# Moving the second layer's products two slots later, with their operands' loads and parts, in a fused attention and feed-forward kernel

## The chip, the cores and the metric

The kernel runs on one core of one Trainium2 chip. The metric is the device time of one execution in microseconds (us). Engines are called as in the profile: PE (TensorE matmuls), PEld (TensorE's weight loads), DVE (VectorE), ACT (ScalarE), POOL (GpSimd) and SP (SyncE, which issues nearly all DMAs here). `L627` is line 627 of the kernel before.

## What is computed

```python
scores = (1 / S) * z @ z.transpose(0, 2, 1)      # z: 4 x 3008 x 64
attn = np.maximum(scores, 0.0) ** 2
x = (u * (attn @ v)).reshape(12032, 256)         # u, v: 4 x 3008 x 256
gate = 1 / (1 + np.exp(-(x @ w_gate)))           # w_gate, w_val: 256 x 1536
out = (gate * (x @ w_val)) @ w_out               # w_out: 1536 x 256
```

Everything is computed to nearly full fp32 by splitting each operand into a high and a low part; a product then takes three matmuls (high by high, high by low, low by high).

## The kernel before, in words

The order of the whole program is written out by hand. There is no planner: the instructions stand on each engine in the order in which the Python code calls the helpers, and two tables put side work into that order. `before` and `after` hold side work of the attention by step number `g` (run just ahead of or behind the step's own work), and `extra` holds side work of the feed-forward part by `(J, slot)`.

**Attention, 0 to about 905 us.** 288 steps: 4 batches, 6 chunks of queries (512, the last 448), 12 pairs of key blocks; `per` = 72 steps are one batch. A step takes scores on PE (L343, L344), squares them on ACT, makes a high part `ah` (ACT, L367) and a low part `al` (DVE, L372) and multiplies with v (`pe_pv`, L487 to L494). As scores are symmetric, some steps don't compute them but load those of an earlier step, which were transposed on DVE and stored to DRAM (`store_turned`, L398, L403; `load_back`, L461, issued five steps ahead). All of these DMAs go through SP's one queue, in program order. Beside the steps run: the next batch's z (`load_z`, `turn_z` on DVE two steps later, `z_high` on ACT at L262 and `z_low` on DVE at L266 one step after that); 18 `Narrow` jobs that prepare the weights and store them to DRAM (L227); the stores of attention's result, `keep` (copy L512, DMA L510). In the last batch (g from 216 on) the feed-forward part's first operands are fetched too: `load_w` (L604, 896 KB each), `load_sums` (L545), `load_u` (L556, eight DMAs each), `turn_u` and `make_x` (DVE).

**Feed-forward, from about 891 us.** 12 groups `G` of 1024 tokens (the last of 768), `NF` = 6 pairs of blocks of the hidden width; `J` = 6 G + F numbers the 72 blocks. A block has a gate half and a value half. Each half is seven products of Strassen's scheme (`pe_product`, L627 to L629, three matmuls each, in the order P1, P6, P2, P7, P5, P4, P3), which go round the PSUM banks 0 to 3. A block has eight slots, 0 to 7, after P6, P7, P5 and P3 of the gate half and then of the value half. In each slot `beside(J, slot)` puts one product of the second layer (`pe_out`, L685 to L687, three matmuls) of the block before, in the order of the quarters 11, 22, 21, 12, twice each, and then what `extra` holds for the slot. So a block is 42 + 24 = 66 matmuls.

The other engines serve a block in this order. ACT: `copy_s1` (L646) out of PSUM, sigmoids (`gate`, L656), the high parts of the hidden values (`h_high`, L664). DVE: `join` (L652), which adds PSUM banks up and frees them. POOL: `gated` (gate times value, L660) and the low parts of the hidden values (`h_low`, L669). The quarters 22, 21 and 12 of a block are finished early in the next block: `h_low(J-1, 22)` is called before that block's P6 (its operand shows as `al` or `al_69`).

Each group prepares the next one's operand beside its blocks: `load_sums`, `load_u` (L556), `turn_u` (DVE L565), `make_x` (DVE L573), four differences `sum_x` (DVE L583), four high parts `x_high` (ACT L587) and four low parts `x_low` (DVE L592), the last of them in the slots 0 to 3 of the group's sixth block. `finish` (DVE L693, DMA L696) writes a group's output. The second layer's weights come by `load_o` (L611, 512 KB), the value halves' weights by `load_w(J + 2, 1)` ahead of each block.

Of the kernel before, what the change touches and what calls it, by code (L numbers as in the profile page):

```python
# [26 lines left out]
def kernel(  # L27
# [20 lines left out]
    NF = DFF // (2 * P)  # L48
# [652 lines left out]
    with tc.manual_schedule():  # L701
# [13 lines left out]
        for b in range(1, B):  # L715
            g0 = (b - 1) * per
            for p in range(NCH):
# [5 lines left out]
                at(before, g + 3, z_high, b, p)  # L723
                at(before, g + 3, z_low, b, p)
# [12 lines left out]
        starts = [24, 31, *range(84, 127, 7), *range(156, 199, 7), 221, 228]  # L737
# [9 lines left out]
        at(after, g + 2, load_w, 0, 1)  # L747
        at(after, g + 6, load_w, 1, 1)
        for t in range(2):
            at(after, g + 10 + t, load_sums, 0, t)  # L750
        for t in range(2):
            at(after, g + 14 + 10 * t, load_u, 0, t)
            at(before, g + 20 + 10 * t, turn_u, 0, t)
            at(before, g + 21 + 10 * t, make_x, 0, t)
        for J in range(3):
            at(after, g + 28 + 5 * J, load_w, J, 0)
# [108 lines left out]
        for G in range(1, len(groups) + 1):  # L865
            J = (G - 1) * NF
            if G < len(groups):
                for t in range(2):
                    at(extra, (J, 0), load_sums, G, t)
                line = (  # L870
                    (1, 3, load_u, 0), (1, 7, turn_u, 0), (1, 7, load_u, 1), (2, 3, make_x, 0), (2, 7, turn_u, 1),
                    (3, 3, make_x, 1), (3, 4, x_high, B1), (3, 7, x_low, B1),
                    (4, 0, sum_x, T1), (4, 1, sum_x, T3), (4, 3, sum_x, T2), (4, 4, sum_x, T4),
                    (4, 5, x_high, T12), (4, 7, x_low, T12), (5, 0, x_high, T34), (5, 1, x_low, T34),
                    (5, 2, x_high, B2), (5, 3, x_low, B2),
# [3 lines left out]
                for x, (t, h) in enumerate(((0, 0), (0, 1), (1, 0), (1, 1))):  # L879
                    at(extra, (J + NF + (x == 3), (5, 6, 7, 0)[x]), finish, G - 1, t, h)  # L880
        at(extra, (0, -1), load_o, 0)
        at(extra, (0, 1), load_w, 2, 1)
        for J in (3, 4, 5):
            at(extra, (0, 7), load_w, J, 0)
        at(extra, (0, 7), keep, *steps[-1][:2], False)
        at(extra, (0, 7), keep, *steps[-1][:2], True)
        for F in range(1, NF):
            at(extra, (0, 7), load_o, F)
# [8 lines left out]
        def attention():  # L897
            for s in steps[-2:]:
                yield from pe_pv(s)

        other = attention()
# [5 lines left out]
        for J in range(last + 1):  # L907
            run(extra, (J, -1))
            for value in range(2):
# [20 lines left out]
                if J and not value:  # L930
                    h_high(J - 1, 12)
                    h_low(J - 1, 12)
# [4 lines left out]
                beside(J, k + 1)  # L937
                pe_product(J, value, "P5", S1, T12, 0)
# [18 lines left out]
            other = outs(J)  # L957
        gated(last, 12)
        for c in (22, 21, 12):
# [37 lines left out]
```

## Time and profile before

| | us |
|---|---|
| median of 3 runs | 1933.91 (1931.49 to 1935.72) |
| the profiled execution's own time | 1938.98 |
| its span | 1937.2 |

| engine | busy us | share of the span |
|---|---|---|
| PE | 1895.7 | 98% |
| PEld | 1659.7 | 86% |
| DVE | 1514.5 | 78% |
| ACT | 1151.5 | 59% |
| POOL | 765.4 | 40% |

PE is busy nearly always; the mean granted clock of the span is 0.997. A busy share says little here about where the rest is: the waits of PE stand in few places, and the rows further down show them one by one. In a row of the timeline the first number is the start in us from the span's start, the second the duration of one instruction, `x2` the number of instructions drawn together, and the square bracket the idle time just before with what ended it.

### The profile page before, as it was taken

The page shows a single profiled execution, that of the slowest core. Times are in us where ns is not written, and L with a number is a line of the kernel's source. Part 1 is how long each engine was busy: PE and PEld are TensorE (multiplying, and loading weights), DVE is VectorE, ACT ScalarE, POOL GpSimd, SP SyncE. Part 2 cuts the span into 40 slices and gives each one's busy share as a digit, 9 for nine tenths or more (in the row PEclk, how much of TensorE's full clock was granted, in tenths as well). Part 3 has the DMA queues.
Part 4 walks back from the last instruction along what each step waited for, and adds up shares of the span by engine and source line. Part 5 has one row for each costly group of instructions (what it writes and reads, how often), then busy time and mean ns, then how long its engine had stood idle before and what let it go on. Part 6 is the DMA issues. An engine that isn't in the chain of part 4 may idle for free.

```text
span 1937.2 us, 26164 instructions
## 1 busy us (share of the span) xinstructions
PE 1895.7 (98%) x8870; PEld 1659.7 (86%) x8870; DVE 1514.5 (78%) x1946; ACT 1151.5 (59%) x1504; POOL 765.4 (40%) x609
## 2 busy tenths in 40 slices
PE   9999999999999999999899999999999999999998
PEld 7888988888887988889788888888888888888898
DVE  7687688887888797657678787888878787888876
ACT  8886788767886787764344444444444444444443
POOL 3000000000000000002577677777777677777675
PEclk9999999999999999999999999999999999999999
DMA  6679589997899889966342515243442415242331
GB/s 141 144 204 245 161 191 238 253 266 197 203 245 272 250 211 219 271 192 241 98 112 87 122 59 142 80 104 92 104 111 89 115 65 142 79 105 86 99 98 36
DMA packets 596726, 298.77 MB, mean 154 GB/s; under 512 B 529904, under 2 KB 547056, under 8 KB 596592
## 3 DMA queue, kind: packets, MB, share of 16 engines
q1 hardware_dynamic: 591312, 294.48, 57.4%
q0 software_dynamic: 1024, 2.10, 0.5%
q8 instruction: 69, 1.13, 0.2%
q10 hardware_dynamic: 4256, 0.52, 0.2%
q14 instruction: 65, 0.53, 0.1%
HBM read 189.92 MB, written 101.06 MB: 150 GB/s over the span
## 4 chain that ended last, share of the span: by engine, by line
PE 77%; POOL 5%; DVE 4%; issue 4%; DMA 3%; ACT 3%; SPq 3%; DVEq 0%; ACTq 0%; POOLq 0%
PE banks L494 10%; PE banks L487 9%; PE banks L627 9%; PE banks L489 9%; PE banks L629 9%; PE banks L628 9%; PE banks L686 5%; PE banks L687 5%; PE banks L685 5%; POOL keep L660 3%; PE banks L344 3%; PE banks L343 3%; DMA r<-shared 2%; DVE al L372 1%; ACT ah L367 1%
## 5 line engine op out<-in xcount | busy, mean ns | idle before, releaser
L660 POOL TENSOR_TENSOR keep<-keep,spare 128x512 f32<-128x512 f32 (+1 forms) x284 | 377.1, 1339 | 1069.2 <-DVE keep L652 1069.2
L372 DVE TENSOR_TENSOR al<-r,ah 128x1024 fp32r<-128x1024 f32 (+1 forms) x287 | 341.2, 1191 | 181.0 <-ACT ah L367 175.3
L487 PE MATMUL banks<-ah,v 128*128 128x512 f32 (+1 forms) x1152 | 429.5, 376 | 9.6 <-ACT ah L367 9.3
L489 PE MATMUL banks<-ah,v 128*128 128x512 f32 (+1 forms) x1104 | 414.0, 375 | 0.0
L494 PE MATMUL banks<-al,v 128*128 128x512 f32 (+1 forms) x1152 | 341.2, 378 | 5.8 <-DVE al L372 4.0
L367 ACT ACTIVATE ah<-r 128x1024 fp32r<-128x1024 f32 (+1 forms) x251 | 255.9, 1034 | 69.7 <-DMA r<-shared 36.6
L487 PEld LDWEIGHTS banks<-ah,v 128*128 128x128 f32 x1152 | 218.0, 189 | 39.0 <-ACT ah L367 13.1
L494 PEld LDWEIGHTS banks<-al,v 128*128 128x128 f32 x1152 | 215.7, 189 | 40.9 <-DVE al L372 15.9
L652 DVE TENSOR_TENSOR zt<-banks,zt 128x512 f32<-128x512 f32 (+1 forms) x288 | 193.4, 672 | 71.7 <-ACT zt L646 66.8
L664 ACT ACTIVATE h<-keep 128x512 fp32r<-128x512 f32 (+1 forms) x144 | 89.7, 623 | 256.2 <-POOL keep L660 252.8
L656 ACT ACTIVATE spare<-spare 128x512 f32<-128x512 f32 (+1 forms) x288 | 176.0, 619 | 99.0 <-DVE spare L652 94.7
L489 PEld LDWEIGHTS banks<-ah,v 128*128 128x128 f32 x1104 | 209.0, 189 | 24.3
L669 POOL TENSOR_TENSOR h<-keep,h 128x512 fp32r<-128x512 f32 (+1 forms) x144 | 196.9, 1368 | 56.8 <-ACT h L664 56.8
L351 ACT ACTIVATE r<-banks 128x1024 f32<-128x1024 f32 (+2 forms) x173 | 167.1, 966 | 86.0 <-PE banks L344 84.5
L652 DVE TENSOR_TENSOR spare<-banks,zt 128x512 f32<-128x512 f32 (+1 forms) x288 | 188.1, 673 | 19.4 <-PE banks L629 18.4
L352 ACT ACTIVATE r<-r 128x1024 f32<-128x1024 f32 (+2 forms) x173 | 174.4, 1008 | 5.5
L646 ACT ACTIVATE zt<-banks 128x512 f32<-128x512 f32 (+1 forms) x144 | 84.1, 584 | 144.2 <-PE banks L629 138.8
L627 PE MATMUL banks<-z,v 128*128 128x512 f32 x378 | 144.1, 381 | 1.1 <-DVE zt L652 1.1
L629 PE MATMUL banks<-z,v 128*128 128x512 f32 x378 | 143.5, 380 | 0.0
L664 ACT ACTIVATE v<-keep 128x512 fp32r<-128x512 f32 (+1 forms) x144 | 89.1, 619 | 71.6 <-POOL keep L660 69.5
L343 PE MATMUL banks<-zq,z 128*128 128x512 f32 (+2 forms) x348 | 126.9, 367 | 1.4 <-DVE zq L787 1.4
L344 PE MATMUL banks<-zq,z 128*128 128x512 f32 (+2 forms) x348 | 126.8, 367 | 0.0
(156 smaller groups left out, 3785.8 us busy)
## 6 DMA issues: line engine op xcount, KB each, us to landing
v<-w_gv SPq DMA_DIRECT2D x75, 896.0 KB, 4.7
r<-shared SPq DMA_DIRECT2D x72, 512.0 KB, 5.1
shared<-turned SPq DMA_DIRECT2D x236, 128.0 KB, 2.9
r<-shared SPq DMA_DIRECT2D x38, 448.0 KB, 5.2
shared<-spare SPq DMA_DIRECT2D x128, 128.0 KB, 3.4
out_dram<-turned SPq DMA_DIRECT2D x176, 64.0 KB, 1.9
w_gv<-w SPq DMA_DIRECT2D x24, 448.0 KB, 4.1
sums<-keep SPq DMA_DIRECT2D x20, 512.0 KB, 4.4
```

The lines of the kernel that those rows point to most:

```text
L343: nc.tensor.matmul(sc[:, j, 0 : n - q0], h, q, start=True, stop=False)
L344: nc.tensor.matmul(sc[:, j, 0 : n - q0], l, q, start=False, stop=True)
L367: nc.scalar.activation(ah[:, :, 0:n], r[:, :, 0:n], AF.Copy)
L372: nc.vector.tensor_tensor(al[:, :, 0:n], r[:, :, 0:n], f32(ah[:, :, 0:n]), op=ALU.subtract)
L487: nc.tensor.matmul(o, vh[:, j, ds], moving(ah[:, j, 0:n]), start=(k == 0 and j == 0), stop=False)
L489: nc.tensor.matmul(o, vl[:, j, ds], moving(ah[:, j, 0:n]), start=False, stop=False)
L494: nc.tensor.matmul(acc[:, d, 0:n], vh[:, j, ds], moving(al[:, j, 0:n]), start=False, stop=stop)
L627: nc.tensor.matmul(o, wt[:, 0, w], xh, start=True, stop=False)
L629: nc.tensor.matmul(o, wt[:, 1, w], xh, start=False, stop=True)
L652: nc.vector.tensor_tensor(to[:, 0:m], bank(J, value, name), s_t[other][:, 0:m], op=ALU.add)
L660: (nc.vector if J == last else nc.gpsimd).tensor_tensor(y, y, g, op=ALU.mult)
L669: nc.gpsimd.tensor_tensor(lo[:, 0:m], y_t[c][:, 0:m], f32(hi[:, 0:m]), op=ALU.subtract)
```

## The change

All edits move calls; no instruction of the computation is added or removed. They are:

1. The products of the second layer of block J stand in the slots from (J+1, 2) to (J+2, 1), before in (J+1, 0) to (J+1, 7). Ten of them are left behind the last block, before eight; two of these go ahead of the last block's high and low parts. `h_high` and `h_low` of quarter 12 move behind slot 1, and `finish` moves by two slots.
2. In the group before, `load_u`, `turn_u`, `make_x` and the high and low parts of x are spread differently: a high part now stands two slots ahead of its low part or more, and `load_u`'s second half stands four slots later.
3. `load_o(F)` stands in (F-1, 7), and `load_w(F, 0)` of F = 3, 4, 5 in (0, 7), (1, 7), (2, 7); before, all eight stood in (0, 7).
4. In the last batch the two last `Narrow` jobs start at steps 246 and 261 (before 221, 228), `load_u` at 243 and 252 (before 230, 240), and the loads of weights and sums later too.
5. `z_high` and `z_low` of the next batch's z stand one step later.

```diff
@@ -720,8 +720,8 @@
                     g = 5 * NPAIR + 3
                 at(after, g, load_z, b, p)
                 at(before, g + 2, turn_z, b, p)
-                at(before, g + 3, z_high, b, p)
-                at(before, g + 3, z_low, b, p)
+                at(before, g + 4, z_high, b, p)
+                at(before, g + 4, z_low, b, p)
             line = [number[b - 1, NCH - 1, i] for i in range(NPAIR)]
             for i in range(1, NPAIR):
                 line[i] = max(line[i], line[i - 1] + 1)
@@ -734,7 +734,7 @@
             for p in range(NCH):
                 if (b, p) != (0, 0):
                     at(after, b * per + NPAIR * p - 10, z_both, b, p)
-        starts = [24, 31, *range(84, 127, 7), *range(156, 199, 7), 221, 228]
+        starts = [24, 31, *range(84, 127, 7), *range(156, 199, 7), 246, 261]
         for n, g in enumerate(starts):
             job = Narrow(n)
             at(after, g - 3, job.load)
@@ -744,16 +744,16 @@
 
 
         g = 3 * per
-        at(after, g + 2, load_w, 0, 1)
-        at(after, g + 6, load_w, 1, 1)
+        at(after, g + 3, load_w, 0, 1)
+        at(after, g + 9, load_w, 1, 1)
         for t in range(2):
-            at(after, g + 10 + t, load_sums, 0, t)
+            at(after, g + 22 + t, load_sums, 0, t)
         for t in range(2):
-            at(after, g + 14 + 10 * t, load_u, 0, t)
-            at(before, g + 20 + 10 * t, turn_u, 0, t)
-            at(before, g + 21 + 10 * t, make_x, 0, t)
+            at(after, g + 27 + 9 * t, load_u, 0, t)
+            at(before, g + 33 + 9 * t, turn_u, 0, t)
+            at(before, g + 34 + 9 * t, make_x, 0, t)
         for J in range(3):
-            at(after, g + 28 + 5 * J, load_w, J, 0)
+            at(after, g + 55 + 3 * J, load_w, J, 0)
         g = len(steps) - NPAIR
         for i in (T1, T3):
             at(before, g + 2, sum_x, 0, i)
@@ -868,24 +868,23 @@
                 for t in range(2):
                     at(extra, (J, 0), load_sums, G, t)
                 line = (
-                    (1, 3, load_u, 0), (1, 7, turn_u, 0), (1, 7, load_u, 1), (2, 3, make_x, 0), (2, 7, turn_u, 1),
-                    (3, 3, make_x, 1), (3, 4, x_high, B1), (3, 7, x_low, B1),
-                    (4, 0, sum_x, T1), (4, 1, sum_x, T3), (4, 3, sum_x, T2), (4, 4, sum_x, T4),
-                    (4, 5, x_high, T12), (4, 7, x_low, T12), (5, 0, x_high, T34), (5, 1, x_low, T34),
-                    (5, 2, x_high, B2), (5, 3, x_low, B2),
+                    (1, 4, load_u, 0), (2, 3, turn_u, 0), (2, 3, load_u, 1), (2, 7, make_x, 0), (3, 3, turn_u, 1),
+                    (3, 7, make_x, 1), (4, 0, sum_x, T1), (4, 1, x_high, B1), (4, 1, sum_x, T3), (4, 3, x_low, B1),
+                    (4, 4, sum_x, T2), (4, 5, x_high, T12), (4, 5, sum_x, T4), (4, 7, x_low, T12),
+                    (5, 0, x_high, T34), (5, 1, x_high, B2), (5, 3, x_low, T34), (5, 5, x_low, B2),
                 )
                 for dj, slot, f, x in line:
                     at(extra, (J + dj, slot), f, G, x)
                 for x, (t, h) in enumerate(((0, 0), (0, 1), (1, 0), (1, 1))):
-                    at(extra, (J + NF + (x == 3), (5, 6, 7, 0)[x]), finish, G - 1, t, h)
+                    at(extra, (J + NF + (x > 0), (7, 1, 2, 3)[x]), finish, G - 1, t, h)
         at(extra, (0, -1), load_o, 0)
         at(extra, (0, 1), load_w, 2, 1)
-        for J in (3, 4, 5):
-            at(extra, (0, 7), load_w, J, 0)
         at(extra, (0, 7), keep, *steps[-1][:2], False)
         at(extra, (0, 7), keep, *steps[-1][:2], True)
         for F in range(1, NF):
-            at(extra, (0, 7), load_o, F)
+            at(extra, (F - 1, 7), load_o, F)
+        for x, F in enumerate((3, 4, 5)):
+            at(extra, (x, 7), load_w, F, 0)
 
         def outs(J):
 
...
-        def attention():
+        def others():
+
             for s in steps[-2:]:
                 yield from pe_pv(s)
-
-        other = attention()
+            yield
+            yield
+            for J in range(last + 1):
+                yield from outs(J)
+
+        other = others()
...
-                if J and not value:
-                    h_high(J - 1, 12)
-                    h_low(J - 1, 12)
                 pe_product(J, value, "P7", S3, T34, 0)
                 join(J, value, "P7", "u3", "u2")
                 if value:
                     h_low(J, 11)
                 beside(J, k + 1)
+                if J and not value:
+                    h_high(J - 1, 12)
+                    h_low(J - 1, 12)
...
-            other = outs(J)
         gated(last, 12)
+        for _ in range(2):
+            next(other)
```

**SP's queue at the start of the feed-forward part**, before. `w_gv` and `w_o` are the prepared weights in DRAM, `sums` attention's result, `in_u_dram` the input u:

```order
L611 DMA x<-w_o 128x1024
L545 DMA turned<-sums 128x2x512 x2
L604 DMA v<-w_gv 128x1792 x4
L510 DMA sums<-turned 256x1x448
L611 DMA ah<-w_o 128x1024 x3
L611 DMA al<-w_o 128x1024 x2
L604 DMA v<-w_gv 128x1792
L556 DMA turned<-in_u_dram 32x16x32 x16
```

And now:

```order
L611 DMA x<-w_o 128x1024
L545 DMA turned<-sums 128x2x512 x2
L604 DMA v<-w_gv 128x1792
L510 DMA sums<-turned 256x1x448
L611 DMA ah<-w_o 128x1024
L604 DMA v<-w_gv 128x1792 x2
L556 DMA turned<-in_u_dram 32x16x32 x8
L611 DMA ah<-w_o 128x1024
L604 DMA v<-w_gv 128x1792 x2
L556 DMA turned<-in_u_dram 32x16x32 x8
L611 DMA ah<-w_o 128x1024
```

Counted from the first L604, the first eight loads of u stood behind eleven transfers of 448 to 896 KB (five L604, the store L510, five L611); now they stand behind five (three L604, the store, one L611).

**SP's queue in the last batch, second chunk of queries**, before. `shared` and `half` are transposed scores in DRAM, stored by L398 and loaded back by L461 and L454:

```order
L270 DMA zq<-z 64x512
L271 DMA zq<-z 64x512
L556 DMA zt<-in_u_dram 32x16x32 x8
L398 DMA shared_1_3_5660<-turned 32x16x64 x8
L461 DMA r<-shared_0_1_5272 128x1024
L454 DMA r<-half_1_5568 128x2x256
```

And now:

```order
L270 DMA zq<-z 64x512
L271 DMA zq<-z 64x512
L398 DMA shared_1_3_5630<-turned 32x16x64 x8
L461 DMA r<-shared_0_1_5272 128x1024
L454 DMA r<-half_1_5553 128x2x256
```

The eight loads of u that stood ahead of a load of transposed scores are gone from here; the first of them now stand in the third chunk.

**PE in a group's sixth block (J = 5)**, before, from slot 1 to slot 2. `z`, `zq` are the parts of x, `v` the first layer's weights; L685 to L687 are one product of the second layer, whose operands are a quarter of h (`h`, or `v` with `al_69`) and the weights `al`:

```order
L685 MATMUL banks<-h,al 128x512
L686 MATMUL banks<-h,al 128x512
L687 MATMUL banks<-h,al 128x512
L627 MATMUL banks<-z,v 128x512
L628 MATMUL banks<-z,v 128x512
L629 MATMUL banks<-z,v 128x512
L685 MATMUL banks<-v,al 128x512
L686 MATMUL banks<-al_69,al 128x512
L687 MATMUL banks<-v,al 128x512
```

And now, from slot 3 to slot 4:

```order
L685 MATMUL banks<-h,al 128x512
L686 MATMUL banks<-h,al 128x512
L687 MATMUL banks<-h,al 128x512
L627 MATMUL banks<-z,v 128x512
L628 MATMUL banks<-z,v 128x512
L629 MATMUL banks<-z,v 128x512
L627 MATMUL banks<-z,v 128x512
L628 MATMUL banks<-z,v 128x512
L629 MATMUL banks<-z,v 128x512
L685 MATMUL banks<-v,al 128x512
L686 MATMUL banks<-al_69,al 128x512
L687 MATMUL banks<-v,al 128x512
```

The product that reads `al_69`, quarter 22's low part, stood behind P5 of the gate half; it now stands behind P6 of the value half, 18 matmuls later.

## Rows read from the trace of the kernel before

**Rows 1.** Waits view, PE, whole span: line, releaser; us in total, times, longest.

```profile
PE banks L487 <- ACT ah L367: 9.3, 8, 2.7
PE banks L686 <- POOL al L669: 8.0, 11, 0.8
PE banks L627 <- DVE zt L652: 7.9, 11, 5.7
```

**Rows 2.** Timeline, PE, a value half without waits: its first matmul and the next block's.

```profile
1008.69 0.38 PE L627 MATMUL banks<-v 128*128 128x512 f32 x1
...
1015.81 0.38 PE L627 MATMUL banks<-v,wgv 128*128 128x512 f32 x1
```

**Rows 3.** Timeline, start of the feed-forward part: SP's issues, DVE, PE.

```profile
908.69 2.54 SPq L611 DMA_DIRECT2D ah<-w_o  x3
...
916.06 18.31 SPq L556 DMA_DIRECT2D turned<-in_u_dram  x16
...
929.07 1.25 DVE L565 STREAM_TRANSPOSE turned<-turned 128x1024 f32<-128x1024 f32 x1 [8.83 <-DMA turned<-in_u_dram]
...
930.94 0.79 PE L627 MATMUL banks<-z,wgv 128*128 128x512 f32 x1 [5.66 <-DVE zt L652]
```

**Rows 4.** Windows: PE, PEld, DVE, ACT, POOL busy (count), PE clock, DMA share, GB/s.

```profile
750.00:760.00 10.00, 7.12 (x24) 5.36 (x23) 5.54 (x5) 6.65 (x8) 0.00 (x0) 0.83 1.03 255
910.00:920.00 10.00, 10.00 (x48) 8.75 (x47) 7.02 (x11) 3.69 (x6) 5.87 (x6) 1.00 1.00 380
920.00:930.00 10.00, 5.28 (x25) 4.29 (x23) 1.17 (x2) 1.75 (x3) 5.85 (x5) 0.97 0.64 153
930.00:940.00 10.00, 9.06 (x30) 7.48 (x31) 7.73 (x12) 3.60 (x6) 2.14 (x2) 0.69 0.60 144
```

**Rows 5.** Timeline, PE around a group end, J = 5, and the same place a group later.

```profile
971.49 0.38 PE L627 MATMUL banks<-z,v 128*128 128x512 f32 x1
...
977.22 0.48 PE L686 MATMUL banks<-al,al 128*128 128x512 f32 x1 [0.81 <-POOL al L669]
...
980.74 0.48 PE L627 MATMUL banks<-z,v 128*128 128x512 f32 x1 [0.23 <-DVE zt L652]
...
1068.09 0.48 PE L627 MATMUL banks<-x,v 128*128 128x512 f32 x1 [0.22 <-DVE zt L652]
```

**Rows 6.** Timeline, POOL, ACT and DVE in the same block J = 5.

```profile
972.43 3.50 POOL L660 TENSOR_TENSOR keep<-keep,spare 128x512 f32<-128x512 f32 x2
975.89 1.28 POOL L669 TENSOR_TENSOR al<-keep,v 128x512 fp32r<-128x512 f32 x1
...
976.50 1.04 ACT L587 ACTIVATE x<-turned 128x1024 fp32r<-128x1024 f32 x1
...
977.58 1.91 DVE L592 TENSOR_TENSOR x<-turned,x 128x1024 fp32r<-128x1024 f32 x1 [1.93 <-ACT x L587]
```

**Rows 7.** Timeline, POOL and ACT in a block in the middle of a group, J = 8.

```profile
1015.51 2.51 POOL L660 TENSOR_TENSOR keep<-keep,spare 128x512 f32<-128x512 f32 x2
1017.98 1.28 POOL L669 TENSOR_TENSOR al<-keep,v 128x512 fp32r<-128x512 f32 x1
...
1020.53 0.63 ACT L664 ACTIVATE v<-keep 128x512 fp32r<-128x512 f32 x1 [0.50 <-POOL keep L660]
```

**Rows 8.** Timeline, last batch, second chunk: SP's issues and PE.

```profile
737.16 5.75 SPq L556 DMA_DIRECT2D zt<-in_u_dram  x8
...
747.63 0.57 SPq L461 DMA_DIRECT2D r<-shared  x1
...
753.77 0.48 PE L487 MATMUL banks<-ah,v 128*128 128x512 f32 x1 [2.75 <-ACT ah L367]
```

**Rows 9.** Timeline, PE's waits behind the last block.

```profile
1926.52 0.43 PE L686 MATMUL banks<-al,al 128*128 128x384 f32 x1 [0.43 <-POOL al L669]
...
1928.84 0.43 PE L686 MATMUL banks<-h,al 128*128 128x384 f32 x1 [0.84 <-POOL h L669]
```

**Rows 10.** Timeline, ACT, one of the 18 high parts of z.

```profile
170.85 0.61 ACT L262 ACTIVATE z<-zt 128x512 fp32r<-128x512 f32 x1
```

## Prediction

> **What bounds the kernel now.** PE: the table gives it 98% of the span, so only two things can shorten the run, idle time of PE and matmuls that run at less than the full clock. I read the waits view of PE first [rows 1]: three kinds of wait make 25.2 us, and two of the three have a longest one that is far above their mean, so they are single places and not something in every block. Then the spacing of matmuls without waits: a value half is 33 matmuls and takes 1015.81 - 1008.69 = 7.12 us, 0.2158 us each [rows 2]. With this spacing each place can be priced by its loss of matmuls, refill and clock included, not by the wait alone.
>
> *The start of the feed-forward part.* PE stands 5.66 us at 930.94 for a join of DVE. That join stands behind DVE's transpose of u (L565 at 929.07), which was idle 8.83 us for the DMA of u [rows 3]. The u was late because its 16 transfers were issued from 916.06 on, behind the weights that SP had begun to issue by 908.69. Behind the wait PE's granted clock is 0.69 in the mean of 930 to 940, so part of that stretch ran at 1.2 GHz instead of 2.4. By count: 25 + 30 matmuls in 920 to 940 where the full stretch before has 48 in 10 us [rows 4], so 96 - 55 = 41 are missing, 41 x 0.2158 = **8.8 us**.
>
> *The ends of groups.* The same matmul stands at 980.74 and, one group later, at 1068.09 [rows 5]: 87.35 us for 6 x 66 = 396 matmuls, which without waits would take 396 x 0.2158 = 85.45. So 1.90 us are lost in each group. The rows in the group's sixth block show where: L686 waits 0.81 for POOL's low part of quarter 22, and P6 of the value half waits 0.23 for DVE [rows 5]; the other 0.86 I take for the refill behind these waits, since a block without them loses nothing [rows 2]. Of the 8.0 us for which L686 waits on POOL [rows 1] 0.43 stands behind the last block [rows 9]; 7.6 / 0.81 = 9.4 full waits, 9.4 x 1.90 = **17.8 us** in all.
>
> *The last batch.* PE stands 2.75 us at 753.77 for ACT, which had waited for transposed scores; SP issued their load only at 747.63, behind eight loads of u that took it 5.75 us from 737.16 on [rows 8]. 750 to 760 holds 24 matmuls at a mean clock of 0.83 [rows 4] instead of 10 / 0.2158 = 46.3: 22 x 0.2158 = **4.8 us**.
>
> **The change part by part.**
>
> *Weights and u at the start.* The order of SP shows the first eight loads of u behind five transfers, before behind eleven; the six that went are two of 896 KB and four of 512 KB, 3.8 MB. At 380 GB/s, the rate of 910 to 920 [rows 4], that is 10 us. DVE got its data at 929.07, so they can now be there at about 919 to 922. The transposition moves too, from slot 7 of the group's second block to slot 3 of its third, that is four slots or 7.1 us later, so the data have 7 us and more before anyone waits. With DVE's idle time of 8.83 us gone, its join at 930.94 is on time. The loss goes whole: **-8.8**. Nothing takes its place in this stretch that the rows show; what moved behind u are weights that are needed one to four blocks (14.2 us each) later. Bounds: -8.8 and, if u came 4 us late once more, about -4.
>
> *The second layer's products two slots later.* In the sixth block POOL finishes the low part of quarter 22 at 975.89 + 1.28 = 977.17, 5.68 us after the block's start at 971.49 [rows 5, 6]. Its first reader stands behind 21 matmuls: due at 22 x 0.2158 = 4.75, hence the wait. In the new order that reader stands behind the value half's P6: 39 matmuls, due at 40 x 0.2158 = 8.63. The cover is 8.63 - 5.68 = 2.95 us. In the middle of a group the same part is done 1017.98 + 1.28 - 1015.81 = 3.45 us after the start [rows 7], where it had 1.30 us of cover and gets 5.2. So the wait on POOL goes.
>
> *High parts of x two slots ahead.* The wait of 0.23 on DVE stands behind a low part (L592, 1.91 us at 977.58) that had itself waited 1.93 us for ACT's high part (L587, 1.04 us at 976.50) [rows 6]. Now the high part is called two slots or four ahead, a slot being some 1.8 us, so the 1.93 us go and DVE is that much earlier than the 0.23 it lacked. The cost is ACT's: two high parts of 1.04 us stand in slots 0 and 1 of the sixth block instead of 0 and 2, ahead of the copy of P1 that DVE needs for its join. What is late next there is that copy. I can't read its lateness from the rows of before; bounds are 0 and the old small wait with its refill, 0.6 per end. I take 0.35, the nearer to the rows with such a wait: 10 x 0.35 = 3.5. Together with the products: **-17.8 + 3.5 = -14.3**.
>
> POOL was slow in this block: its two products took 3.50 us, in the middle of a group 2.51 [rows 6, 7]. These 0.99 us stay, since a low part of x still runs beside them; they are inside the 5.68. The Trainium skill, "SBUF — State Buffer", section "Who interferes with whom", has a rule that speaks against the change here: a DVE instruction with two SBUF inputs and a GpSimd instruction that reads SBUF exclude each other for the whole instruction, and the one that issued first wins. By that rule each of the low parts and differences may hold POOL once; the trace agrees in kind (3.50 against 2.51). As one more such instruction now stands in the fifth block, the sum by the rule would be worse only if its holds add up beyond the cover; that is the first rival.
>
> *The last batch.* The eight loads of u are gone from ahead of the late load [rows 8], and nothing stands in their place in SP's queue in that chunk. So the load that was issued at 747.63 comes up to 5.75 us earlier, against a wait of 2.75: **-4.8**. The same eight DMAs and the sums now stand in the third and fourth chunk. There I bound them from below by 0 and from above by one more stall like the one that goes, 4.8. I take +1.2, a quarter, for these and for the moved weights and `Narrow` jobs, nearer to 0 because one wait of 2.75 is by far the longest of its eight [rows 1], so other chunks with as many DMAs don't stall.
>
> *z a step later.* 18 high parts of 0.61 us on ACT [rows 10] and as many low parts on DVE move by one step; nothing needs them soon, so the moves themselves cost nothing. Where the new step already has ACT late, 0.61 is added to PE's wait for `ah`. Bounds: 0 and 18 x 0.61 = 11. PE waits for ACT's `ah` in eight places only [rows 1]; I take one of them in each of three batches, once whole and twice by half: **+1.1**.
>
> *Behind the last block.* Two more products, 6 matmuls of 384 columns, are put ahead of the waits of 0.43 and 0.84 [rows 9]. They fill most of the 1.27 us: **-1.0**; the chain on POOL ends it, so no more than 1.27.
>
> Sum: -8.8 - 14.3 - 4.8 + 1.2 + 1.1 - 1.0 = -26.6. The profiled execution took 1938.98, so it would take 1912.4. That execution lay 5.1 above the median of 1933.91; taken off the median, the sum gives 1907.3. **Forecast: 1907 us.**
>
> **The rivals.**
>
> *1. POOL stays the bound at group ends.* The order of the fifth and sixth block still puts six or seven two-input DVE instructions beside POOL's work. If three more of them than now hold POOL for about 0.99 us each, the low part comes 2.97 us later and the cover of 2.95 is used up; from there on each hold shows in PE. Half of the 17.8 would stay: 1907 + 5.4 (8.9 instead of 3.5) = 1912, all of it 1921. Against it: in the rows one hold of 0.99 is all that the block has. This is the page's rule worked out as a mechanism of this kernel.
>
> *2. The u loads stall another chunk.* In the third or fourth chunk of the last batch the eight DMAs (5.75 us of SP) push a load of scores as they did at 737. Each such stall costs 4.8: one gives 1911, two 1915. For it: the queue is the same. Against it: fewer stores stand there.
>
> *3. Slower: ACT waits for PE in every block.* `h_high` of quarter 12 overwrites an operand that PE now reads in slots 0 and 1 of the same block, for the block before. These products end behind 18 matmuls, 3.9 us after the block's start; the high part starts 1020.53 - 1015.81 = 4.72 after it [rows 7], so 0.8 us of margin. If ACT came to be held there by more than the later work of ACT can absorb, three sigmoids and the copy of P1 would be late and PE would wait in each of about 70 blocks. To eat up the gains it must cost 30 / 70 = 0.43 us per block; at 0.7 per block the time is 1907 + 49 = 1956. Against it: the margin is positive, and ACT is busy 59%.
>
> *4. The change doesn't do what it says.* If the join at 930.94 and the group ends were held by something beside POOL and u, both would stay: about 1931. The order shows the products and the loads moved as described, and the rows name POOL and the DMA with no other engine late, so this is small.
>
> **How the numbers follow.** Chances: forecast 0.76, first rival 0.10, second 0.06, third 0.04, fourth 0.04. The range should leave out at most 2 in 10. Its upper end takes in the second rival twice and most of the first: 1919. Its lower end: all 17.8 gone without the 3.5, nothing lost in z and the moved loads (2.3), gives 1907.3 - 5.8 = 1901.5, and with 3 us for the spread of the three runs 1898. A change of about 0.2%, 4 us, is what a measurement of this kernel can tell from none. Faster by more: forecast and rivals one and two, 0.92; within: 0.04; slower: 0.04.
>
> **What would show it.** In the waits of PE: no wait of 5 us near 930 and a clock of 1.00 in 920 to 940; L686 no longer waiting on POOL at the ends of groups, a period of 85.5 to 85.9 us between like matmuls of two groups; P6's wait on DVE below 0.3. In the last batch: no wait of 2 us or more for `ah` near 753 and none new in the two chunks after it. Wrong would be the forecast if the period stayed above 86.5, if L487 waited for ACT by more than 8 us in all, or if a wait of a few tenths stood in every block.

## The result

The changed kernel takes 1912.55 us (median of 4 runs, 1910.79 to 1913.78) where the kernel before takes 1934.82 (4 runs, 1931.49 to 1938.16): a ratio of 0.9884, with an interval of 0.9865 to 0.9904, so 22.3 us less. The forecast was 1907, the range 1898 to 1919. The profiled execution took 1912.1, its span is 1910.3, 26.9 less than the span of before.

PE's waits of the changed kernel (line, releaser; us in total, times, longest), which answer to [rows 1]:

```profile
PE banks L487 <- ACT ah L367: 6.0, 5, 2.1
...
PE banks L686 <- POOL h L669: 0.8, 1, 0.8
```

L627 on DVE (7.9 us before) and L686 on POOL in the groups (7.6 us before) are gone; what is left on POOL is the one wait behind the last block. The windows that answer to [rows 4]:

```profile
750.00:760.00 10.00, 10.00 (x48) 8.81 (x48) 4.58 (x5) 8.90 (x10) 0.00 (x0) 1.00 0.93 234
...
920.00:930.00 10.00, 10.00 (x48) 8.78 (x47) 8.65 (x13) 3.27 (x7) 5.75 (x6) 1.00 0.62 159
930.00:940.00 10.00, 10.00 (x49) 8.75 (x48) 8.48 (x12) 5.07 (x9) 7.49 (x6) 1.00 0.65 263
```

Both bad stretches are full: 48 or 49 matmuls at a granted clock of 1.00 where 24, 25 and 30 stood. The timeline shows why at the start of the feed-forward part [rows 3]; u's first half is issued 9.83 us earlier (5.9 us earlier counted from the first matmul of the feed-forward part, which stands at 888.19 here and at 892.09 before), and its transposition has no idle time ahead:

```profile
904.42 0.96 SPq L604 DMA_DIRECT2D v<-w_gv  x2
906.23 8.06 SPq L556 DMA_DIRECT2D turned<-in_u_dram  x8
...
922.08 1.23 DVE L565 STREAM_TRANSPOSE turned<-turned 128x1024 f32<-128x1024 f32 x1
```

At a group's end, J = 11, with the fifth block, J = 10, ahead of it, PE and POOL [rows 5, 6]:

```profile
1036.87 0.38 PE L629 MATMUL banks<-v 128*128 128x512 f32 x1
1037.24 0.48 PE L627 MATMUL banks<-x,v 128*128 128x512 f32 x1
...
1044.26 0.38 PE L629 MATMUL banks<-v 128*128 128x512 f32 x1
1044.61 0.48 PE L627 MATMUL banks<-x,v 128*128 128x512 f32 x1
...
1052.70 0.38 PE L686 MATMUL banks<-al,al 128*128 128x512 f32 x1
...
1123.32 0.48 PE L627 MATMUL banks<-z,v 128*128 128x512 f32 x1
```

```profile
1044.80 3.51 POOL L660 TENSOR_TENSOR keep<-keep,spare 128x512 f32<-128x512 f32 x2
1048.27 1.28 POOL L669 TENSOR_TENSOR al<-keep,v 128x512 fp32r<-128x512 f32 x1
```

POOL is as slow as before (3.51 against 3.50), its low part is ready at 1049.55, and PE reads it only at 1052.70: 3.15 us of cover, 2.95 by the prediction. Like matmuls of two groups are 1123.32 - 1037.24 = 86.08 us apart, before 87.35, and 85.45 would be without any loss. The period that the prediction gave was 85.5 to 85.9. The remaining 0.6 stand mostly in two places of like size: P6 of the fifth block's value half follows the matmul ahead of it after 0.37 us instead of 0.22 (1036.87 to 1037.24) and P6 of the sixth block's gate half after 0.35 (1044.26 to 1044.61); the matmul behind each comes 0.32 later, so each place loses some 0.25.

### The profile page after: what moved, and what is told of

The parts are those of the page before. It is cut to its first block, busy times and chain, and to the rows that moved or that the text cites. A ratio compares the mean times of both kernels' runs of the same rounds, so it can differ in the third digit from the quotient of the medians.

```text
span 1910.3 us, 26147 instructions
## 1 busy us (share of the span) xinstructions
PE 1889.4 (99%) x8870; PEld 1662.3 (87%) x8870; DVE 1531.9 (80%) x1946; ACT 1145.5 (60%) x1504; POOL 778.6 (41%) x609
## 4 chain that ended last, share of the span: by engine, by line
PE 90%; ACT 2%; SPq 2%; DVE 2%; DMA 2%; issue 1%; DVEq 0%; POOL 0%; ACTq 0%
PE banks L627 11%; PE banks L628 11%; PE banks L629 11%; PE banks L494 11%; PE banks L487 10%; PE banks L489 10%; PE banks L686 6%; PE banks L687 6%; PE banks L685 6%; PE banks L344 3%; PE banks L343 3%; DMA r<-shared 1%; SPq L252 1%; ACT ah L367 1%; DVE al L372 1%
## 5 line engine op out<-in xcount | busy, mean ns | idle before, releaser
L660 POOL TENSOR_TENSOR keep<-keep,spare 128x512 f32<-128x512 f32 (+1 forms) x284 | 387.3, 1374 | 1036.1 <-DVE keep L652 1032.0
L669 POOL TENSOR_TENSOR h<-keep,h 128x512 fp32r<-128x512 f32 (+1 forms) x144 | 188.1, 1307 | 56.8 <-ACT h L664 56.8
L652 DVE TENSOR_TENSOR spare<-banks,zt 128x512 f32<-128x512 f32 (+1 forms) x288 | 188.2, 674 | 22.5 <-PE banks L629 21.4
L627 PE MATMUL banks<-z,v 128*128 128x512 f32 x378 | 144.4, 382 | 0.0
```

The lines of the kernel that those rows point to most:

```text
L627: nc.tensor.matmul(o, wt[:, 0, w], xh, start=True, stop=False)
L652: nc.vector.tensor_tensor(to[:, 0:m], bank(J, value, name), s_t[other][:, 0:m], op=ALU.add)
L660: (nc.vector if J == last else nc.gpsimd).tensor_tensor(y, y, g, op=ALU.mult)
L669: nc.gpsimd.tensor_tensor(lo[:, 0:m], y_t[c][:, 0:m], f32(hi[:, 0:m]), op=ALU.subtract)
```

## Experiments

The kernels were compared with the kernel before on the same chip; its medians there were 1934.6 to 1935.6. Experiments one to four each do one part of the change alone.

**The products two slots later, alone.** The edit is the generator `others` with its two empty slots, the parts of quarter 12 behind slot 1, and:

```diff
-at(extra, (J + NF + (x == 3), (5, 6, 7, 0)[x]), finish, G - 1, t, h)
+at(extra, (J + NF + (x > 0), (7, 1, 2, 3)[x]), finish, G - 1, t, h)
```

> The kernel before with the second layer's products two slots later (and the finish and quarter 12's parts that go with them), nothing else of the change. Theory: POOL's late low part is the cause of the loss at group ends, so the waits of L686 on POOL (10 of 0.8 us) go and of the 1.90 us per group only P6's wait on DVE with its refill stays, about 0.5; with the tail 14 us less than before, about 1921. Rival: DVE is as late as POOL there, so PE only reaches P6 earlier and the wait of L627 on DVE grows from 0.23 to about 1.3 per group; then no more than 5 us are won, 1930 or more. The wait of 5.7 us at 931 stays in both.

Measured: 1953.3, ratio 1.0100 (1.0072 to 1.0129). It is 18.7 us slower. PE's waits, the same place at two group ends, and the third block:

```profile
PE banks L627 <- DVE zt L652: 29.6, 21, 5.2
```

```profile
978.25 0.48 PE L627 MATMUL banks<-z,v 128*128 128x512 f32 x1 [1.37 <-DVE zt L652]
...
1019.53 0.48 PE L627 MATMUL banks<-x,wgv 128*128 128x512 f32 x1 [0.87 <-DVE zt L652]
...
1066.79 0.48 PE L627 MATMUL banks<-x,v 128*128 128x512 f32 x1 [1.38 <-DVE zt L652]
```

The wait of L686 on POOL in the groups is gone, as the first theory said, but at the group's end nothing is won: P6 now waits 1.37 us for DVE instead of 0.23, as the rival said. Neither had foreseen the third block, where a new wait stands. DVE there, in this run and then in the kernel before, and SP in this run:

```profile
1017.66 1.25 DVE L565 STREAM_TRANSPOSE turned<-turned 128x1024 f32<-128x1024 f32 x1 [4.03 <-DMA turned<-in_u_dram]
```

```profile
1016.90 1.25 DVE L565 STREAM_TRANSPOSE turned<-turned 128x1024 f32<-128x1024 f32 x1 [0.79 <-DMA turned<-in_u_dram]
```

```profile
1003.88 7.59 SPq L696 DMA_DIRECT2D out_dram<-turned  x12
1011.52 11.44 SPq L556 DMA_DIRECT2D turned<-in_u_dram  x16
```

The later products make `finish` later (its first quarter by two slots, the other three by three), and the twelve stores of these three stand right ahead of u's loads in SP's queue. Counted from the group's first matmul, the loads are issued at 26.7 us (1011.52 - 984.83), before at 21.4 (1008.75 - 987.32). So u comes late, and DVE idles 4.03 us instead of 0.79. With both waits the group takes 1066.79 - 978.25 = 88.54 us.

**The operands of x, alone.** The edit is the table of `load_u` to `x_low`.

> The kernel before with u's loads, its transposition, the differences and the high and low parts of x at their new slots, nothing else. Theory: at group ends P6's wait on DVE goes (0.5 us with its refill, 10 times) and L686's wait on POOL stays at 0.8, so 5 us less there. At the start of the feed-forward part u lands no earlier than before (929), but its transposition is due four slots or 7.1 us later, at about the time at which the data are there, so the wait of 5.7 us falls under 1.5 and the clock stays up: 7 to 8.5 us less. In all about 1921. Rival: the weights ahead in SP's queue are what counts, and u stays late: a wait of 4 us or more on DVE's transposition near 930 stays, and the time is about 1929.

Measured: 1926.0, ratio 0.9958 (0.9945 to 0.9970), 8.6 us less; the profiled execution took 1928.5. PE and DVE:

```profile
971.14 0.48 PE L686 MATMUL banks<-al,al 128*128 128x512 f32 x1 [0.62 <-POOL al L669]
...
1057.99 0.48 PE L686 MATMUL banks<-al,al 128*128 128x512 f32 x1 [0.61 <-POOL al L669]
```

```profile
929.99 1.25 DVE L565 STREAM_TRANSPOSE turned<-turned 128x1024 f32<-128x1024 f32 x1 [0.19 <-DMA turned<-in_u_dram]
```

P6's wait is gone and POOL's stays; the group takes 86.85 us, 0.5 less than before, as expected. The wait at 931 is gone too, although u comes hardly earlier (transposed at 929.99, 35.5 us behind the first matmul of the feed-forward part, before at 929.07, 37.0 behind it): with its use four slots later DVE is idle for 0.19 us instead of 8.83. At the prices read from the profiled execution of before these two would be 13 us, and 1921 was expected; the median shows 8.6. The next experiment prices the second of them lower, which is most of the rest.

**The weights spread, alone.** The edit:

```diff
-for J in (3, 4, 5):
-    at(extra, (0, 7), load_w, J, 0)
...
-    at(extra, (0, 7), load_o, F)
+    at(extra, (F - 1, 7), load_o, F)
+for x, F in enumerate((3, 4, 5)):
+    at(extra, (x, 7), load_w, F, 0)
```

> The kernel before with the second layer's weights and three of the first layer's spread over the blocks, nothing else. Theory: u's loads stand behind five transfers instead of eleven and land about 10 us earlier (919 to 922), DVE's idle time of 8.8 us goes, the wait of 5.7 us goes with its half clock: 8.5 us less, about 1926. Rival: the weights share the DMA engines with u either way, u comes less than 4 us earlier, and 3 us or more of the wait stay. The group ends keep their 1.9 us each in both.

Measured: 1929.6, ratio 0.9970 (0.9958 to 0.9982), 5.1 us less. DVE's transposition:

```profile
923.31 1.25 DVE L565 STREAM_TRANSPOSE turned<-turned 128x1024 f32<-128x1024 f32 x1 [0.95 <-DMA turned<-in_u_dram]
```

u is transposed 5.8 us earlier than before (929.07), or 7.9 us earlier counted from the first matmul of the feed-forward part (894.21 here, 892.09 before), and that suffices: no wait of PE is left there. The gain is smaller than the forecast, though: 8.5 us less were expected, and 5.1 came, with 3.5 to 8.1 in the interval. So either the spread of the weights or the later use of u cures the start of the feed-forward part by itself, the changed kernel has both, and the whole wait is worth less in the medians than the 8.8 us read from one trace.

**The last batch, alone.** The edit is the new steps of `load_w`, `load_sums`, `load_u`, `turn_u`, `make_x` and of the two last `Narrow` jobs.

> The kernel before with the last batch's loads and the two last Narrow jobs at their new steps, nothing else. Theory: the wait of 2.75 us at 754 and its half clock go (4.8 us), so do the 0.44 at 809 and its refill (1.1), and one new wait of 0.9 us near 850 comes: 5 us less, about 1929. Rival: u's loads stall one of the two later chunks: a new wait of 2 us or more for ah between 780 and 880, and no gain.

Measured: 1931.8, ratio 0.9979 (0.9968 to 0.9991), 2.9 us less. The window that was bad, and the start of the feed-forward part:

```profile
750.00:760.00 10.00, 10.00 (x48) 8.83 (x47) 5.90 (x6) 8.29 (x9) 0.00 (x0) 1.00 0.89 232
```

```profile
921.86 0.79 PE L627 MATMUL banks<-z,wgv 128*128 128x512 f32 x1 [3.68 <-DVE zt L652]
```

The stall near 754 is gone, and neither of the two later chunks has one of 2 us; the rival falls. The new wait of 0.9 us near 850 did not come. At the start of the feed-forward part, where SP's queue has the same order as before, PE waits 3.68 us, before 5.66. The stall near 754 was not the same in each execution: in the three runs above, which keep the old last batch, PE's wait there was 2.97, 3.71 and 3.46 us, and in two below 1.30 and 2.56. The 2.75 us of the prediction's trace lie in the middle of these, so the term was right in place, and its size varies with the execution.

**Products and u.** The products later, and u's loads, transposition and product at their new slots, but the parts of x at their old ones:

```diff
-(1, 3, load_u, 0), (1, 7, turn_u, 0), (1, 7, load_u, 1), (2, 3, make_x, 0), (2, 7, turn_u, 1),
-(3, 3, make_x, 1), (3, 4, x_high, B1), (3, 7, x_low, B1),
+(1, 4, load_u, 0), (2, 3, turn_u, 0), (2, 3, load_u, 1), (2, 7, make_x, 0), (3, 3, turn_u, 1),
+(3, 7, make_x, 1), (3, 4, x_high, B1), (3, 7, x_low, B1),
```

> The kernel before with the products two slots later and u's loads, transposition and product four slots later, but the differences and the high and low parts of x at their old slots. In the run with the products alone two waits of L627 on DVE stood in each group: 1.4 us at the group's end, and 0.4 to 2.4 in its third block, where DVE was idle 4.0 us for u. Theory: they are two things. The third block's goes, since u gets four slots more; the group's end keeps its 1.4 us, which hang on the high part that ACT makes only one slot ahead of the low part; with the start of the feed-forward part cured too (8.5) the time is about 1925, and like matmuls of two groups lie 87.2 us or more apart. Rival: both come from the late u, the group's end gets within 0.6 of 85.45, and the time is about 1913.

Measured: 1953.4, ratio 1.0090 (1.0069 to 1.0111). One group of PE's timeline:

```profile
953.07 0.48 PE L627 MATMUL banks<-z,v 128*128 128x512 f32 x1 [0.63 <-DVE spare L652]
956.60 0.48 PE L627 MATMUL banks<-z,v 128*128 128x512 f32 x1 [1.31 <-DVE zt L652]
972.47 0.48 PE L627 MATMUL banks<-z,v 128*128 128x512 f32 x1 [1.36 <-DVE zt L652]
```

DVE ahead of the same waits a group later (PE's stand there at 1042.63 and 1046.15):

```profile
1036.24 1.83 DVE L573 TENSOR_TENSOR turned<-turned 128x1024 f32<-128x1024 f32 x1
1038.00 2.29 DVE L592 TENSOR_TENSOR z<-turned,z 128x1024 fp32r<-128x1024 f32 x1
```

The third block's wait is gone and the group's end keeps its 1.36, so these are two things, as the theory said. The time of 1925 was wrong all the same, for a reason that this edit itself made: the product by u and B1's low part now stand in the same slot, right ahead of two differences; DVE has no idle time there, and PE waits for it twice in the fifth block (953.07 and 956.60).

**Products and all operands.** The two parts together; weights, last batch and z as before.

> The kernel before with the products later and all of u's and x's operands at their new slots; second layer's weights, last batch and z as before. Theory: these two parts make the whole gain of the feed-forward part, which each of them alone does not: group period 86.1 as in the changed kernel, no wait at its start; only the last batch's stall of some 5 us is left, so 1916 to 1918. Rival: the weights' spread is needed too, and a wait of 2 us or more is left between 915 and 935: 1920 or more.

Measured: 1914.8, ratio 0.9893 (0.9870 to 0.9916). PE's waits on DVE:

```profile
PE banks L627 <- DVE zt L652: 1.3, 2, 1.0
```

Both stand in the first group: 1.00 us at 929.53 and 0.33 in the sixth block (961.50). From the second group on no wait on POOL or DVE is left, but for the one on POOL behind the last block. The theory is borne out (1916 to 1918 expected, the time 1 us lower): two parts that are worth +18.7 and -8.6 alone are worth -20.8 together.

**The parts of x one slot apart again.** The changed kernel with:

```diff
-(5, 0, x_high, T34), (5, 1, x_high, B2), (5, 3, x_low, T34), (5, 5, x_low, B2),
+(5, 0, x_high, T34), (5, 1, x_low, T34), (5, 2, x_high, B2), (5, 3, x_low, B2),
```

> The changed kernel with one thing put back: in a group's sixth block each low part of x stands one slot behind its high part again (T34 in slots 0 and 1, B2 in slots 2 and 3). Theory: the other half of the loss at group ends is DVE, which stands idle for ACT's high part while PE waits for DVE; so P6's wait of 1.4 us with its refill is back at each end, a period of 87.3, 12 us more than the changed kernel, 1924. Rival: what made the difference was the less dense order of the differences in the fifth block; then the wait stays away and the time is 1912 to 1914.

Measured: 1926.0, ratio 0.9946 (0.9926 to 0.9967), 13.4 us above the changed kernel's 1912.55 (12.0 by the two ratios). PE, then DVE and ACT:

```profile
967.84 0.48 PE L627 MATMUL banks<-z,v 128*128 128x512 f32 x1 [1.12 <-DVE zt L652]
...
1055.22 0.48 PE L627 MATMUL banks<-x,v 128*128 128x512 f32 x1 [1.13 <-DVE zt L652]
```

```profile
964.67 1.92 DVE L592 TENSOR_TENSOR x<-turned,x 128x1024 fp32r<-128x1024 f32 x1 [0.99 <-ACT x L587]
966.51 0.68 DVE L652 TENSOR_TENSOR spare<-banks,spare 128x512 f32<-128x512 f32 x1
967.11 0.68 DVE L652 TENSOR_TENSOR zt<-banks,zt 128x512 f32<-128x512 f32 x1
```

```profile
963.60 1.04 ACT L587 ACTIVATE x<-turned 128x1024 fp32r<-128x1024 f32 x1
```

The wait is back and the group takes 87.38 us. The chain can be read off: ACT's high part ends at 964.64, DVE's low part waits for it and takes 1.92, two joins follow, and PE's P6 waits for the bank that the second frees.

**The products one slot later instead of two.** The changed kernel with one empty slot in `others`:

```diff
 yield from pe_pv(s)
-yield
 yield
 for J in range(last + 1):
```

> The changed kernel with the second layer's products one slot later than before instead of two. By the prediction's sum quarter 22's low part is ready 5.68 us after the block's start and is now due behind 30 matmuls, at 31 x 0.2158 = 6.69: a cover of 1.0 us, so no wait of L686 on POOL and the same time as the changed kernel, 1912. Rival: POOL is held by more in the denser order of DVE (more two-input instructions beside it), the low part comes later than 6.7, and waits on POOL are back at group ends: 0.5 us or more each with refill, 1918 or more.

Measured: 1918.9, ratio 0.9914 (0.9891 to 0.9938); the profiled execution took 1915.9. POOL and PE in the sixth block:

```profile
961.58 1.28 POOL L669 TENSOR_TENSOR al<-keep,v 128x512 fp32r<-128x512 f32 x1
```

```profile
964.34 0.38 PE L686 MATMUL banks<-al,al 128*128 128x512 f32 x1
```

Ready at 962.86, read at 964.34: 1.48 us of cover where 1.0 was expected, and no wait on POOL. So one slot is enough against POOL. The time is not that of the changed kernel, though: PE stands idle for 0.13 us ahead of L685 at 990.97, until DVE's `finish` has ended (0.71 us from 990.21), as `finish` kept its place while its reader came a slot earlier, and like matmuls of two groups, 990.97 and 1077.53, are 86.56 us apart. Ten groups, from the first matmul of block 6 to that of block 66, take 863.0 us in this profiled execution and 859.7 in that of the changed kernel. These 3.3 us are about half of the difference of the medians; where the rest stands is not settled.

**z at its old step.** The changed kernel with `g + 3` for `z_high` and `z_low`.

> The changed kernel with z's parts back at their old step. Theory of the prediction: the later z costs 1.1 us, so 1.1 less than the changed kernel, 1911.4. First rival: it costs more, since in the changed kernel a wait of 0.9 us is new at 380 and those at 401 and 622 are 0.2 longer: 2 to 3 us less, about 1910. Second rival: it gains, since waits of 1.2 us at 446 and of 0.5 at 404 and 626 are gone there: 2 to 3 us more, about 1915.

Measured: 1912.6, ratio 0.9878 (0.9859 to 0.9896).

> The changed kernel once more, beside the others of this call: 1912.5 within 1.5.

Measured, beside it: 1911.2, ratio 0.9872 (0.9850 to 0.9894). So the step of z makes no difference that these runs can tell; the two rivals of 2 to 3 us either way aren't borne out.

**DVE's side work spread further.** The changed kernel with z at its old step and `make_x` of the first half in slot 6 instead of 7, and this table behind it:

```diff
+(2, 7, x_high, B1), (3, 1, x_low, B1), (3, 3, turn_u, 1), (3, 5, make_x, 1), (3, 6, x_high, B2), (4, 0, x_low, B2),
+(4, 2, sum_x, T1), (4, 4, sum_x, T3), (4, 6, sum_x, T2), (4, 7, x_high, T12), (5, 0, sum_x, T4),
+(5, 1, x_low, T12), (5, 2, x_high, T34), (5, 4, x_low, T34),
```

> The changed kernel with z's parts at their old step and DVE's side work for the next operand spread further: B2's parts in the fourth and at the start of the fifth block, T1, T3 and T2 two slots apart, T4 in the sixth. Theory: what the changed kernel still loses per group (86.08 against 85.45 us) are joins of DVE in the fifth block that come late behind a product and two differences in four slots; one such piece in every two slots leaves DVE time for its joins, the 0.6 us go in each of 11 groups, 6 us less than the changed kernel, 1906. Rival: the pieces meet POOL's work at their new places, DVE is late there, and the time is 1912 or more.

Measured: 1922.0, ratio 0.9928 (0.9910 to 0.9946), 9.4 us above the changed kernel with z at its old step (1912.6): the rival's time. PE waits for DVE again in the sixth block:

```profile
PE banks L627 <- DVE keep L652: 2.5, 10, 0.2
```

This wait stands in the value half, behind T34's low part, which now has the slot ahead of that join:

```profile
1143.10 1.22 DVE L592 TENSOR_TENSOR x<-turned,x 128x1024 fp32r<-128x1024 f32 x1
1144.23 0.69 DVE L652 TENSOR_TENSOR keep<-banks,zt 128x512 f32<-128x512 f32 x1
```

```profile
1144.97 0.48 PE L627 MATMUL banks<-z,v 128*128 128x512 f32 x1 [0.25 <-DVE keep L652]
```

The value half's P6 waits too in some groups, up to 0.64 us (at 965.33), for joins that stand behind T12's low part (2.34 us at 961.74, with POOL at work).

**The product by u earlier.** The changed kernel with two calls moved:

```diff
-(3, 7, make_x, 1), (4, 0, sum_x, T1),
+(3, 5, make_x, 1), (3, 7, sum_x, T1),
```

> The changed kernel with x's second product by u two slots earlier (from slot 7 to slot 5 of the fourth block) and the first difference T1 one slot earlier (slot 7 of the fourth block). Theory: the 0.6 us that the changed kernel still loses per group stand in the fifth block, where DVE works off that product, which met POOL there (1.84 us), and three differences without idle time; between them and slot 5 DVE has idle time and POOL none to give, so DVE's backlog is some 1.8 us less, the group period falls from 86.1 to about 85.6, and the time by 4 to 5 us, 1907 to 1908. Rival: DVE's backlog in the fifth block is made by the differences and the joins alone; the period stays at 86, the time at 1912.

Measured: 1908.0 (1906.2 to 1909.3), ratio 0.9854 (0.9837 to 0.9871). Like matmuls two groups apart:

```profile
1062.69 0.38 PE L628 MATMUL banks<-zq,wgv 128*128 128x512 f32 x1
...
1233.63 0.38 PE L628 MATMUL banks<-zq,wgv 128*128 128x512 f32 x1
```

That is 170.94 / 2 = 85.47 us per group: what the matmuls alone take. The median lies below both kernels' (1934.8; 1912.6 and 1911.2) and below every run of the changed one (1908.9 at the lowest). The intervals of the two ratios to the kernel before still overlap, so the size of the gain over the changed kernel is open; that the loss in the groups is gone is what the period shows. DVE there:

```profile
1028.32 1.87 DVE L573 TENSOR_TENSOR turned<-turned 128x1024 f32<-128x1024 f32 x1
...
1032.51 0.68 DVE L583 TENSOR_TENSOR turned<-turned 128x512 f32<-128x512 f32 x1
...
1035.46 0.68 DVE L583 TENSOR_TENSOR turned<-turned 128x512 f32<-128x512 f32 x1
```

The product takes as long as in the changed kernel, but it begins two slots earlier, and the two differences behind it, T1 and T3, take 0.68 us each; in the changed kernel they took 1.16 and 1.81. So DVE is ahead by its earlier start and by these 1.6 us; which of the two counts for more isn't tested.

## Why the prediction was right

The range held the time, the likeliest case was the one that came, and no rival did. Term by term:

| term | forecast | shown |
|---|---|---|
| start of the feed-forward part | -8.8 | wait and low clock gone; two edits each cure it alone, one of them for -5.1 (-3.5 to -8.1) |
| group ends | -14.3 | ten groups, block 6 to block 66: 871.5 to 859.7 us, -11.8; with the first group's end some -13 |
| last batch's stall | -4.8 | gone; with the next row -2.9 (-1.7 to -6.2) in the part alone |
| moved loads and jobs | +1.2 | one new wait of 0.87 us, at 843, in the changed kernel |
| z a step later | +1.1 | none that can be told |
| behind the last block | -1.0 | 34 matmuls take 6.48 us where 28 took 6.44: some -0.9 |

**What was too large.** The sum was 26.6, and the two profiled spans differ by 26.9, but the medians by 22.3, with 18.6 to 26.1 in the interval (24.4 in the repeat). Between the two profiled executions even the parts come out: attention is 3.9 us shorter (forecast 2.5), the group ends some 13 (14.3). The step that made the gain too large is the last: the sum of the terms of one profiled execution was taken off the median. That execution took 1938.98; 23 runs of the same kernel beside the first experiments had a median of 1934.63 and went from 1931.05 to 1939.32. So it lay near the upper end. The term that the runs price lower is the start of the feed-forward part: the weights alone take its wait away whole and gain 5.1 us, not 8.8. With the same order of SP's queue PE waited there 5.66 us in that execution, 5.22 with the products alone (at 928.78) and 3.68 with the last batch alone. The first group, from the first matmul of block 0 to that of block 6, took 95.23 us before and 92.09 with the last batch alone:

```profile
892.09 0.38 PE L627 MATMUL banks<-z,wgv 128*128 128x512 f32 x1
...
987.32 0.38 PE L627 MATMUL banks<-v,wgv 128*128 128x512 f32 x1
```

```profile
884.99 0.38 PE L627 MATMUL banks<-z,wgv 128*128 128x512 f32 x1
...
977.08 0.38 PE L627 MATMUL banks<-v,wgv 128*128 128x512 f32 x1
```

The last batch's stall, on the other hand, wasn't unusually long in that execution (2.75 us, others 1.30 to 3.71), and the part alone agrees with its two terms (-3.6) within its interval. A term that varies like this needs to be counted as a mean over executions, which one trace can't give. Why the wait at the start varies is not settled; with the last batch alone, the loads that this edit moved may have had a share in it.

**What was right by a reason that was too short.** The prediction read the group's end as two waits, 0.81 on POOL and 0.23 on DVE, and put all but 0.6 of the 1.90 us on POOL. The part alone shows that this price was wrong: with POOL's wait gone PE comes to P6 earlier and stands there for DVE, 1.37 us instead of 0.23, and nothing is won. The two are chains side by side, both about as late, and the small wait was small only because PE had been held before it. The forecast came out since the change shortens both; for the products alone the same reasoning gave 1921 and the chip 1953. It also took the moved `finish` as free: the prediction didn't ask what its stores are put ahead of in SP's queue. Alone that cost a wait of 0.4 to 2.4 us in most groups; in the change, `load_u` moved by a slot and u's use by four, and cover it.

**The residue of 0.35 per end** was laid on ACT's copy of P1. It was 0.63 in the groups that had it, and the period of 86.08 lay above the range of 85.5 to 85.9. It stood at P6 of the fifth block's value half and of the sixth block's gate half, which wait for joins of DVE; in the fifth block these come behind a product and two differences without idle time. Moving that product by two slots and T1 by one took all of it away. In the changed kernel the differences there were long as well; the rows of DVE are the product, T1 and T3, and T1 and T3 took 0.68 us each where the product began earlier:

```profile
1029.53 1.84 DVE L573 TENSOR_TENSOR turned<-turned 128x1024 f32<-128x1024 f32 x1
...
1031.89 1.16 DVE L583 TENSOR_TENSOR turned<-turned 128x512 f32<-128x512 f32 x1
...
1034.17 1.81 DVE L583 TENSOR_TENSOR turned<-turned 128x512 f32<-128x512 f32 x1
```

**The first and the third rival.** The Trainium skill, "SBUF — State Buffer", section "Who interferes with whom", lets DVE's two-input instructions and POOL's reads hold each other up. The runs agree in kind: differences of one shape on DVE took 0.68, 1.16 or 1.81 us beside different work of POOL. What the rule could have cost did not come. POOL's two products took 3.51 us in the changed kernel too, and 3.50 before, in blocks with such work of DVE, against 2.51 in a middle block [rows 7]; no further hold came on top, and the cover of 2.95 us (3.15 measured) held, so the first rival stayed away. The third rival, a wait of ACT in every block, would show as 70 waits; the waits view has none in the groups.

## What to carry to other kernels

Where PE waits for two engines one after the other, the second wait can be what the first one leaves of it (here 0.23 us became 1.37): price an edit that removes the first by the lateness of the second engine, read from when its instruction could run, not by the length of its wait. A set of moves may be worth much together and be harmful one by one; before any is dropped or kept alone, ask what the other was covering, queues included. And a trace is one execution: stalls that hang on a DMA vary from run to run, so take their mean, not the one in the trace.

## What the runs showed that was not expected

The step that delays the products costs 18.7 us alone and brings 12 us on top of the operands' new slots (8.6 us less than before without it, 20.8 with it). A store of outputs that moved by a few us in one DMA queue held up loads behind it by enough to idle DVE for 4.03 us, where it had idled for 0.79.
